# Retention and a two-layer network on one core: what two groups of loads wait for

## Chip, cores, metric

The kernel runs on one core of one Trainium2 chip. The time is the device time of one execution in microseconds (us); the median of several executions is given. A core has five engines: TensorE (PE; its weight loads are listed apart as PEld), VectorE (DVE), ScalarE (ACT), GpSimd (Pool) and SyncE (SP), which issues most of the DMA transfers.

## What is computed

The inputs are q, k and v of shape 4 x 8 x 768 x 64 (batch, heads, sequence, head size), w_in (512 x 2048), w_out (2048 x 512) and alpha (2048), all in fp32. A retention layer feeds a two-layer network:

```
state = gamma[head] * state + outer(k[t], v[t])      # for t = 0..767, per batch and head
y[t]  = (1 / 8) * q[t] @ state                        # gamma[head] = 1 - 2 ** (-5 - head)
x = y as 3072 x 512                                   # token by (head, feature)
h = x @ w_in
g = max(h, 0) + alpha * min(h, 0)
out = g @ w_out                                       # 3072 x 512, fp32
```

## The kernel before

**Units and blocks.** The sequence of each batch is cut into pieces of 256 tokens: 12 units. Two units make a block of 512 tokens, and the network runs block by block, 6 in all.

**A unit** goes through these steps. `load(u)` (L107) issues DMAs on SP that bring k, q and v into staging tiles `ks`, `qs`, `vs` with four buffers each; k and q of units 0 to 3 come in halves of four heads, those of later units whole. `rescale` (L135) multiplies k and q by powers of gamma and writes them as fp16 into `kdq`, on VectorE (V) or on Pool (G); `cast_v` (L148) writes v as fp16. `kdq` is then transposed into `kq`: on TensorE for units 0 to 3 (`turn_pe`, L160, evicted by ScalarE at L174), by a DMA transpose that SP issues for the later ones (`turn_dma`, L156). `score_mm` (L241) multiplies k and q, `masks` (L260) multiplies the two banks of scores by the causal mask on VectorE, one instruction for each bank, `sum_mm` (L190) and `state` (L213) carry the state forward (adding on VectorE, L225; decay on Pool, L226; copies on Pool or ScalarE, L239 and L237), and `out_mm` (L271) makes y, which ScalarE writes into `xT`.

**A block of the network** is `ffn1` (L323: matmuls at L334, ScalarE at L345, VectorE at L347) and `ffn2` (L357: matmuls at L366, eviction on ScalarE at L375, output DMA on SP at L379). Both are generators: `tick(gen, m)` issues the next m of their matmuls, so that the code states by hand which matmul stands between which steps of the units. `ffn2(0)` runs in four parts: its first 16 matmuls use only the first quarter of w_out, the next 16 the second quarter, and so on.

**Weights.** `get_wi` and `get_wo` (L418, L422) issue the weights' DMAs on Pool, which cast fp32 to fp16 on the way. w_out comes in four pieces: `get_wo(0)` to `get_wo(3)`, 512 KB each as written.

**What a load waits for.** `held` is a list with at most one instruction; `hold` (L96) lets the next DMA that `load` issues wait until that instruction has finished (a DMA: until it has landed). Since SP issues in order, the rest of that load, and all that stands behind it on SP, waits too. In the stretch concerned the order on SP is: load(2), load(3), load(4), load(5), transpose of unit 4, load(6), four outputs of block 0, transpose of unit 5, load(7). On Pool it is, among rescales and state copies: get_wo(0), get_wo(1), the rest of unit 2, the state's work of unit 2, get_wo(2), a rescale of unit 3 (`rescale(G, 3, 1, 0, 4)`), get_wo(3), the rest of unit 3, the state's work and the rescales of unit 4 and so on.

Before the change, load(3) is held by get_wo(1) (L504), and load(4), with load(5) behind it, by get_wo(3) (L530).

Of the kernel before, what the change touches and what calls it, by code (L numbers as in the profile page):

```python
# [20 lines left out]
def kernel(  # L21
# [10 lines left out]
    nc = tc.nc  # L32
# [61 lines left out]
    held = []  # L94

    def hold(ins):  # L96
        if held:
            tc.add_manual_dep(
                ins.ins,
                held.pop().ins.name,  # L100
                mybir.DependencyInfo(
                    mybir.DependencyClass.Sync, mybir.DependencyReason.DATA
                ),
                reason="loads behind weights",
            )

    def load(u, parts="kqv"):  # L107
        b, c = divmod(u, UPB)
        t = staged.setdefault(u, {})
        for nm in parts:  # L110
            src = {"k": k, "q": q, "v": v}[nm[0]]
            if nm[0] not in t:
                t[nm[0]] = sbp.tile(
                    [128, H, 2 * D], FP, tag=f"{nm[0]}s", bufs=4, name=f"{nm[0]}s{u}"
                )
            h = slice(0, H) if len(nm) == 1 else slice(4 * int(nm[1]), 4 * int(nm[1]) + 4)
            hold(
                nc.sync.dma_start(  # L118
                    out=t[nm[0]][:, h, :],
                    in_=src[b, h, U * c : U * c + U, :].rearrange(  # L120
                        "h (p r) d -> p h (r d)", r=2
                    ),
                )
            )
# [10 lines left out]
    def rescale(eng, u, t, h0, h1):  # L135
        kdq = unit(u)[0]
        at = OQ * t
        eng.tensor_tensor(  # L138
            out=kdq[:, t, :, h0:h1, :].rearrange("p r h d -> p h r d"),
            in0=staged[u]["kq"[t]][:, h0:h1, :].rearrange("p h (r d) -> p h r d", r=2),  # L140
            in1=tab[:, at + 2 * h0 : at + 2 * h1]
            .rearrange("p (h r) -> p h r", r=2)
            .unsqueeze(3)
            .to_broadcast([128, h1 - h0, 2, D]),
            op=MULT,
        )
# [13 lines left out]
    def turn_pe(u, hh, bank):  # L160

        kdq, kq, _ = unit(u)
        trb = ps(bank, "trb", F16, 1024)
        n = 0
        for t in range(2):
            for r in range(2):
                for p in (2 * hh, 2 * hh + 1):
                    nc.tensor.transpose(  # L168
                        out=trb[:, n : n + 128],
                        in_=kdq[:, t, r, 2 * p : 2 * p + 2, :].rearrange("p a d -> p (a d)"),  # L170
                        identity=ident,
                    )
                    n += 128
        nc.scalar.activation(  # L174
            out=kq.rearrange("p (x a) i -> p x a i", x=4)[:, :, 2 * hh : 2 * hh + 2, :],
            in_=trb.rearrange("p (x a i) -> p x a i", x=4, a=2),
            func=COPY,
            bias=0.0,
            scale=1.0,
        )  # L180
# [60 lines left out]
    def score_mm(u, hh, banks):  # L241
        _, kq, _ = prepped[u]
        kv = kq.rearrange("p (t r a) i -> p t r a i", t=2, r=2)
        scs = [ps(banks[0], "sca"), ps(banks[1], "scb")]
        for r in range(2):
            for pp in range(2):
                p = 2 * hh + pp
                for c in range(2):
                    for a in range(2):
                        at = 256 * r + 128 * pp  # L250
                        nc.tensor.matmul(  # L251
                            out=scs[a][rows(c), at : at + 128],
                            lhsT=kv[rows(a), 0, r, p, rows(c)],
                            rhs=qmove(kq, a, c, p),
                            start=True,
                            stop=True,
                        )
        live[u, hh] = scs

    def masks(u, hh, parts=(0, 1)):  # L260
        for a in parts:
            m2 = sbp.tile([128, 2, 2, 128], F16, tag=f"m2{a}{hh}", bufs=2, name=f"m2{a}{hh}")
            nc.vector.tensor_tensor(  # L263
                out=m2,
                in0=live[u, hh][a].rearrange("p (r a i) -> p r a i", r=2, a=2),
                in1=mask.unsqueeze(2).to_broadcast([128, 2, 2, 128]),
                op=MULT,
            )
            live[u, hh][a] = m2

    def out_mm(u, banks, evict=True):  # L271
        _, kq, vx = prepped[u]
        ys = [ps(banks[0], "y0"), ps(banks[1], "y1")]
        inter = [(u, c) in tgs for c in range(2)]
        assert inter == [u % UPB > 0, True]

        for c in range(2):
            for p in range(NP):
                if inter[c]:
                    nc.tensor.matmul(  # L280
                        out=ys[c][:, 128 * p : 128 * p + 128],
                        lhsT=tgs[u, c][:, p, :],
                        rhs=kq.rearrange("p (t r a) i -> p t r a i", t=2, r=2)[
                            :, 1, :, p, rows(c)
                        ],
                        start=(p == 0),
                        stop=False,
                        skip_group_check=True,
                    )
        for p in range(NP):  # L290
            m2s = live[u, p // 2]
            for r in range(2):
                for c in range(2):
                    for a in range(2):
                        nc.tensor.matmul(  # L295
                            out=ys[c][rows(a), 128 * p : 128 * p + 128],
                            lhsT=vx[rows(c), 2 * p + a, r, :],
                            rhs=m2s[a][rows(c), r, p % 2, :],
                            start=(r == 0 and p == 0 and not inter[c]),
                            stop=(r == 1),  # L300
                            skip_group_check=True,
                        )
        live[u] = ys
        if evict:
            take_y(u, (0, 1))
# [116 lines left out]
    def get_wo(i):  # L422
        s = slice(4 * i, 4 * i + 4)
        return nc.gpsimd.dma_start(out=w_out_all[:, s, :], in_=wo[:, s, :])
# [22 lines left out]
    for t in tgbuf:  # L447
# [16 lines left out]
        out=aps[:, 0:NFT], in_=alpha_sb, identity=tab[0:NFT, OI : OI + NFT]  # L464
    )
    masks(0, 0)
    V.tensor_scalar(
        out=oma_sb, in0=aps[:, 0:NFT], scalar1=-1.0, scalar2=1.0, op0=MULT, op1=ADD
# [4 lines left out]
    sum_mm(0, (6, 7))  # L473
    keep(4, 1)
    masks(0, 1, (0,))
    state(0, 0, V, "aa")
    masks(0, 1, (1,))
    s01 = state_sum(0, 1, G)
    held.append(get_wi(4, 8))
# [21 lines left out]
    keep(5, 6)  # L501
    get_wo(0)
    rescale(G, 2, 0, 0, 4)
    held.append(get_wo(1))  # L504
    load(3, ("k0", "q0", "k1", "q1", "v"))
    rescale(G, 2, 1, 0, 4)
    rescale(G, 2, 0, 4, 8)
    rescale(G, 2, 1, 4, 8)
# [8 lines left out]
    turn_pe(2, 0, 5)  # L517
    tick(gen, 5)
    score_mm(2, 0, (6, 7))
    masks(2, 0)  # L520
    turn_pe(2, 1, 4)
    tick(gen, 8)
    score_mm(2, 1, (6, 7))
    sum_mm(2, (5, 4))
    state(2, 0, G, "ga")
    masks(2, 1)
    get_wo(2)
    rescale(V, 3, 0, 0, 4)
    rescale(G, 3, 1, 0, 4)
    held.append(get_wo(3))  # L530
    load(4)
    load(5)
    rescale(V, 3, 0, 4, 8)
    rescale(G, 3, 1, 4, 8)
    cast_v(G, 3)
# [99 lines left out]
```

## Time and profile before

| | |
|---|---|
| median of 3 runs | 212.51 us (212.19 to 213.4) |
| the profiled execution | 212.42 us |
| its span, first to last instruction | 210.7 us |
| TensorE matmuls busy in the span | 202.3 us (96%) |
| VectorE, ScalarE, Pool busy | 119.5, 98.7, 80.5 us |
| DMA moved | 33.91 MB, 161 GB/s on average |

The profile is that of one execution. Times in it count from its first instruction. A row of the timeline gives start, duration, engine, line, operation, output and inputs, count, and in brackets how long the engine had been idle and what ended that; rows with a count above 1 are merged. "SPq" and "POOLq" are the sequencers that issue DMAs; a DMA's row there is its issue, not its transfer. "issue to landing" is the time from the issue until the data is there. In the DMA views q1 is the queue of SP's transfers and q0 that of Pool's; shares are of all 16 DMA engines and can come out a little over 100%.

### The profile page before, as it was taken

The numbers are of one execution on the slowest core, as the hardware profiler recorded it, in microseconds if no ns is written. First come the engines' busy times: TensorE is split into PE (matmuls) and PEld (weight loads), VectorE is DVE, ScalarE is ACT, GpSimd is POOL, SyncE is SP. The second block draws the span as 40 slices with busy tenths as digits, with TensorE's granted clock in tenths as the row PEclk, the third lists the DMA queues.
The fourth block names the chain that finished last, engine by engine and source line by source line (L and its number), as shares of the span: only waits on it lengthen the run. The fifth ranks groups of instructions, "written<-read, shape, count | busy, mean of one in ns | idle before, by whom it ended". The sixth has DMA issues, their size and how long they took to land.

```text
span 210.7 us, 4991 instructions
## 1 busy us (share of the span) xinstructions
PE 202.3 (96%) x2090; PEld 106.4 (50%) x2090; DVE 119.5 (57%) x196; ACT 98.7 (47%) x160; POOL 80.5 (38%) x102
## 2 busy tenths in 40 slices
PE   7789999989999999999999999999999999999993
PEld 2457545574564555444555444555444555444462
DVE  7785985554288731488750488740588640588000
ACT  2375665361666133666133566133665133665121
POOL 2388055630793699000499300499000610000000
PEclk9999999999999999999999999999999999999999
DMA  6999997994999997599521699421630111100112
GB/s 163 335 226 149 202 281 153 261 189 100 344 248 281 306 277 250 145 288 260 159 101 53 152 294 270 154 82 53 172 78 0 52 55 50 50 0 3 50 71 79
DMA packets 62406, 33.91 MB, mean 161 GB/s; under 512 B 18080, under 2 KB 59440, under 8 KB 62384
## 3 DMA queue, kind: packets, MB, share of 16 engines
q1 hardware_dynamic: 57840, 29.30, 49.0%
q0 software_dynamic: 4224, 4.19, 12.6%
q8 instruction: 16, 0.26, 0.5%
q10 hardware_dynamic: 320, 0.10, 0.3%
q14 instruction: 6, 0.05, 0.1%
HBM read 27.30 MB, written 6.29 MB: 159 GB/s over the span
## 4 chain that ended last, share of the span: by engine, by line
PE 82%; DMA 10%; POOL 2%; DVE 2%; SPq 1%; ACT 1%; issue 1%; DVEq 0%; POOLq 0%
PE hps L334 38%; PE ops L366 33%; DMA wout<-in_moe_w_out_dram 4%; DMA kq<-kdq 3%; PE y L295 2%; DMA ks<-in_k_dram 2%; PE sca L251 2%; PE ops L389 2%; PE y L280 2%; PE st L201 2%; SPq L118 1%; POOL tf L226 1%; DVE ss L225 1%; PE scb L251 1%; PE kps L87 1%
## 5 line engine op out<-in xcount | busy, mean ns | idle before, releaser
L347 DVE SCALAR_TENSOR_TENSOR gt<-hm,oma,hps 128x512 f16<-128x512 f32 (+1 forms) x108 | 73.0, 687 | 47.7 <-ACT hm L345 38.7
L366 PE MATMUL ops<-wout,gt 128*128 128x512 f16 x368 | 83.7, 379 | 0.8 <-DMA wout<-in_moe_w_out_dram 0.8
L334 PE MATMUL hps<-xT,win 128*128 128x512 f16 (+1 forms) x432 | 84.3, 355 | 0.0
L345 ACT ACTIVATE hm<-hps 128x512 f32<-128x512 f32 x96 | 57.3, 597 | 26.4 <-PE hps L334 26.3
L334 PEld LDWEIGHTS <-win 128*128 128x128 f16 x432 | 42.2, 98 | 40.7
L366 PEld LDWEIGHTS <-gt 128*128 128x128 f16 x368 | 34.5, 98 | 41.1 <-issue 0.9
L375 ACT ACTIVATE os<-ops 128x512 f32<-128x512 f32 x23 | 13.6, 598 | 52.3 <-PE ops L366 52.3
L226 POOL TENSOR_TENSOR tf<-ss,tab 128x256 f32<-128x256 f32 x16 | 10.2, 637 | 42.4 <-DVE ss L225 41.8
L263 DVE TENSOR_TENSOR m<-sca,mi 128x512 f16<-128x512 f32 x24 | 16.4, 684 | 17.1 <-PE scb L251 17.1
L239 POOL CAST tg<-tf 64x256 f16<-64x256 f32 x35 | 13.8, 394 | 25.7 <-DVE tf L222 24.0
L313 ACT ACTIVATE xT<-y 128x512 f16<-128x512 f32 x24 | 16.2, 740 | 11.1 <-PE y L295 11.1
L138 POOL TENSOR_TENSOR kdq<-qs,tab 128x1024 f16<-128x1024 f32 (+1 forms) x13 | 20.4, 1569 | 1.8 <-DMA qs<-in_q_dram 1.7
L138 POOL TENSOR_TENSOR kdq<-ks,tab 128x1024 f16<-128x1024 f32 (+1 forms) x10 | 17.3, 1728 | 9.4 <-DMA ks<-in_k_dram 9.1
L263 DVE TENSOR_TENSOR m<-scb,mi 128x512 f16<-128x512 f32 x24 | 16.3, 679 | 0.0
L154 POOL CAST vx<-vs 128x1024 f16<-128x1024 f32 (+1 forms) x13 | 12.6, 971 | 7.5 <-DMA vs<-in_v_dram 7.5
L174 ACT ACTIVATE kq<-trb 128x1024 f16<-128x1024 f16 x8 | 8.2, 1023 | 5.4 <-PE trb L168 5.2
L225 DVE TENSOR_TENSOR ss<-tf,st 128x256 f32<-128x256 f32 x16 | 6.6, 414 | 5.6 <-PE st L201 4.7
L251 PE MATMUL sca<-kq 64*64 64x128 f16 x192 | 8.2, 218 | 1.5 <-ACT kq L174 1.3
L87 PE MATMUL kps<-spin 128*128 128x512 f16 x25 | 7.7, 443 | 1.8 <-DVE spin L432 1.5
L251 PEld LDWEIGHTS <-kq 64*64 64x64 f16 x384 | 6.1, 106 | 4.6 <-ACT kq L174 3.0
L251 PE MATMUL scb<-kq 64*64 64x128 f16 x192 | 8.3, 219 | 0.0
L295 PE MATMUL y<-m,vx 64*64 64x128 f16 x384 | 7.7, 219 | 0.0
(33 smaller groups left out, 69.1 us busy)
## 6 DMA issues: line engine op xcount, KB each, us to landing
out_dram<-os SPq DMA_DIRECT2D x23, 256.0 KB, 2.1
vs<-in_v_dram SPq DMA_DIRECT2D x10, 512.0 KB, 6.7
ks<-in_k_dram SPq DMA_DIRECT2D x8, 512.0 KB, 4.4
qs<-in_q_dram SPq DMA_DIRECT2D x8, 512.0 KB, 5.3
ks<-in_k_dram SPq DMA_DIRECT2D x8, 256.0 KB, 4.4
qs<-in_q_dram SPq DMA_DIRECT2D x8, 256.0 KB, 4.6
win<-in_moe_w_in_dram POOLq DMA_DIRECT2D x4, 512.0 KB, 6.6
wout<-in_moe_w_out_dram POOLq DMA_DIRECT2D x4, 512.0 KB, 9.0
```

Source lines behind the costliest of these rows:

```text
L138: eng.tensor_tensor(out=kdq[:, t, :, h0:h1, :].rearrange("p r h d -> p h r d"), in0=staged[u]["kq"[t]][:, h0:h1, :].rearrange("p h (r d) - ...
L154: eng.tensor_copy(out=o, in_=i)
L226: eng.tensor_tensor(out=t, in0=ss, in1=dec, op=MULT)
L239: nc.gpsimd.tensor_copy(out=o, in_=i)
L251: nc.tensor.matmul(out=scs[a][rows(c), at : at + 128], lhsT=kv[rows(a), 0, r, p, rows(c)], rhs=qmove(kq, a, c, p), start=True, stop=True,)
L263: nc.vector.tensor_tensor(out=m2, in0=live[u, hh][a].rearrange("p (r a i) -> p r a i", r=2, a=2), in1=mask.unsqueeze(2).to_broadcast([128, ...
L313: nc.scalar.activation(out=xT[n][:, ul, :, 128 * c : 128 * c + 128].rearrange("k a (p r) -> k a r p", r=2), in_=ys[c].rearrange("k (a r p) ...
L334: nc.tensor.matmul(out=hps[:, f, :].rearrange("p (u t) -> p u t", t=U), lhsT=w_in_all[:, hp, 128 * (f0 + f) : 128 * (f0 + f) + 128], rhs=x ...
L345: nc.scalar.activation(out=hm, in_=hps, func=RELU, bias=0.0, scale=-1.0)
L347: nc.vector.scalar_tensor_tensor(out=gt[:, f0 + f, U * lo : U * hi], in0=hm[:, f, :], scalar=oma_sb[:, f0 + f : f0 + f + 1], in1=hps[:, f, :],
L366: nc.tensor.matmul(out=opss[tq], lhsT=gt[:, ft, 128 * tq : 128 * tq + 128], rhs=w_out_all[:, ft, :], start=(ft == 0), stop=(ft == NFT - 1),)
L375: nc.scalar.activation(out=os_sb, in_=opss[tq], func=COPY, bias=0.0, scale=1.0)
```

## The change

load(3) is no longer held by `get_wo(1)` but by VectorE's first mask instruction of unit 2, and its call stands behind that mask. load(4) and load(5) are held by `get_wo(2)` instead of `get_wo(3)`, and their calls stand between those two pieces. `masks` returns its last instruction for this purpose. No instruction is added or removed, and the order on SP, on Pool and on VectorE stays what it was.

```diff
@@ masks
-            nc.vector.tensor_tensor(
+            i = nc.vector.tensor_tensor(
...
             live[u, hh][a] = m2
+        return i
@@ the first block
     rescale(G, 2, 0, 0, 4)
-    held.append(get_wo(1))
-    load(3, ("k0", "q0", "k1", "q1", "v"))
+    get_wo(1)
     rescale(G, 2, 1, 0, 4)
...
     score_mm(2, 0, (6, 7))
-    masks(2, 0)
+    held.append(masks(2, 0, (0,)))
+    load(3, ("k0", "q0", "k1", "q1", "v"))
+    masks(2, 0, (1,))
     turn_pe(2, 1, 4)
...
     masks(2, 1)
-    get_wo(2)
+    held.append(get_wo(2))
+    load(4)
+    load(5)
     rescale(V, 3, 0, 0, 4)
     rescale(G, 3, 1, 0, 4)
-    held.append(get_wo(3))
-    load(4)
-    load(5)
+    get_wo(3)
     rescale(V, 3, 0, 4, 8)
```

## Prediction

> **What bounds the kernel now.** I read the page first: its span, and TensorE's share of it.
>
> ```profile
> span 210.7 us, 4991 instructions
> ...
> PE 202.3 (96%) x2090; PEld 106.4 (50%) x2090; DVE 119.5 (57%) x196; ACT 98.7 (47%) x160; POOL 80.5 (38%) x102
> ```
>
> TensorE (PE) is busy for 202.3 of 210.7 us, so only its idle time can be won. The change neither adds nor removes an instruction, so it can only move idle time. Where is there some after the start-up? The view by stages (columns: stretch, its length, busy time of each engine with its count, clock, DMA share, GB/s) says:
>
> ```profile
> 34.00:48.00 14.00, 13.18 (x173) 8.74 (x162) 7.78 (x15) 6.89 (x10) 6.23 (x8) 1.00 0.89 192
> 48.00:77.00 29.00, 28.80 (x372) 15.82 (x373) 16.15 (x29) 12.75 (x22) 17.55 (x21) 1.00 0.97 254
> 77.00:206.00 129.00, 129.00 (x1197) 64.19 (x1187) 68.68 (x102) 58.94 (x98) 38.99 (x45) 1.00 0.42 123
> ```
>
> PE idles 0.82 us in 34 to 48, 0.20 us in 48 to 77, and nothing from 77 to 206. Two waits must be behind this. The view of waits between 30 and 80 us (total, times, longest) names them, the last two rows being one wait, seen by the weight loads and by the matmuls:
>
> ```profile
> PE ops L366 <- DMA wout<-in_moe_w_out_dram: 0.8, 1, 0.8
> ...
> PEld L251 <- DMA kq<-kdq: 0.4, 1, 0.4
> PE sca L251 <- DMA kq<-kdq: 0.2, 1, 0.2
> ```
>
> The chain that ended last (start, us, what) passes through both:
>
> ```profile
> 38.44 0.34 POOL tg L239
> 38.78 8.83 DMA wout<-in_moe_w_out_dram
> ...
> 69.66 6.94 DMA kq<-kdq
> ```
>
> The first is w_out's third piece, get_wo(2): issued at 38.78, once Pool has copied a state, and landed at 38.78 + 8.83 = 47.61. The second is unit 5's DMA transpose, issued by SP at 69.66, landed at 76.60. What each costs is read from the timeline of PE (start, us, engine, line, operation, count):
>
> ```profile
> 44.90 0.62 PE L168 MATMUL trb<-mi,kdq 128*128 128x128 f16 x8
> 45.35 1.04 PE L334 MATMUL hps<-xT,win 128*128 128x256 f16 x8
> 46.23 0.61 PE L168 MATMUL trb<-mi,kdq 128*128 128x128 f16 x8
> 47.65 2.10 PE L366 MATMUL ops<-wout,gt 128*128 128x512 f16 x9 [0.82 <-DMA wout<-in_moe_w_out_dram]
> ...
> 50.31 1.90 PE L366 MATMUL ops<-wout,gt 128*128 128x512 f16 x8
> ```
>
> Eight transposes take 45.35 - 44.90 = 0.45 us of the array when nothing stops what follows. After the second eight, L366 could start at 46.23 + 0.45 = 46.68; it starts at 47.65. **Stall 1 costs 0.97 us.** For stall 2 I take the weight loads' 0.4 us, since matmuls can't start before their weights; so unit 5's transposed tile is due at 76.64 - 0.4 = 76.24 and comes 0.4 us late.
>
> **Part 1: load(3) is held by a mask instead of by w_out's second piece.** SP's timeline, and VectorE's first mask of unit 2:
>
> ```profile
> 36.27 0.37 SPq L118 DMA_DIRECT2D ks<-in_k_dram  x1
> ...
> 50.17 0.37 SPq L118 DMA_DIRECT2D ks<-in_k_dram  x1
> ...
> 59.43 3.56 SPq L158 DMA_TRANSPOSE kq<-kdq  x1
> ...
> 65.32 4.24 SPq L379 DMA_DIRECT2D out_dram<-os  x4
> 69.66 4.21 SPq L158 DMA_TRANSPOSE kq<-kdq  x1
> ```
>
> ```profile
> 34.26 0.69 DVE L263 TENSOR_TENSOR m<-sca,mi 128x512 f16<-128x512 f32 x1 [0.65 <-PE scb L251]
> ```
>
> The mask ends at 34.26 + 0.69 = 34.95, so load(3) goes out at about 35.0 instead of 36.27: all its five DMAs 1.27 us earlier, in the same order. Behind the waiting DMA SP has only load(4) and load(5), which wait longer anyway, and no work ahead of the mask needs load(3). The second piece, which loses its waiter, has landed by 36.27, when load(3) is now let go.
>
> An earlier unit 3 gives PE nothing directly: no wait for unit 3 stands in the rows above. What it does is end its traffic 1.27 us earlier, and there stands the third piece. Traffic by queue, q1 being SP's and q0 Pool's (packets, MB, share of 16 engines), first from 29.99 to 32.00, then from 39.00 to 42.00:
>
> ```profile
> q1 hardware_dynamic: 1387, 0.70, 114.9%
> q0 software_dynamic: 2, 0.00, 0.3%
> ```
>
> ```profile
> q1 hardware_dynamic: 1764, 0.88, 101.6%
> ```
>
> In the first stretch the second piece was already issued and q0 moved 2 packets while unit 2's loads filled the engines. In the second the third piece had been issued at 38.78, and q0 has no row at all: from 39 to 42 only load(3) moves. Twice a piece of w_out begins when the load ahead of it has drained. So I let the third piece begin, and land, 1.27 us earlier: 47.61 - 1.27 = 46.34, against the 46.68 at which PE wants it. The price from both sides: nothing won, if the piece starts late for another reason; 0.97 won, if it is on time. It can't win more, since PE arrives at 46.68 either way. I take **0.97**, the end nearest to the two rows, with 0.34 us to spare.
>
> The Trainium skill speaks against this: "DMA: Bandwidth & Descriptors", section "Queues, rings and completion order", says that each DMA engine takes turns between the queues that have work, a packet at a time. By it the third piece would have moved between load(3)'s packets from the start, load(3)'s lead would bring it little, and the sum would be near rival A's. The row of 39 to 42 has no packet of q0, so the trace so far does not show such turns.
>
> **Part 2: load(4) and load(5) are held by the third piece instead of the fourth.** Pool's order doesn't change: get_wo(2), a rescale of unit 3, get_wo(3), as load() issues on SP alone. Pool's timeline:
>
> ```profile
> 40.90 0.80 POOL L424 DMA_DIRECT2D wout<-in_moe_w_out_dram  x1
> ...
> 51.83 0.39 POOL L239 CAST tg<-tf 64x256 f16<-64x256 f32 x1 [5.12 <-DVE tf L222]
> 54.05 1.90 POOL L138 TENSOR_TENSOR kdq<-ks,tab 128x1024 f16<-128x1024 f32 x1 [1.83 <-DMA ks<-in_k_dram]
> ...
> 57.50 1.90 POOL L138 TENSOR_TENSOR kdq<-qs,tab 128x1024 f16<-128x1024 f32 x1
> ```
>
> load(4) now leaves SP at 50.17 and its k lands in time for Pool at 54.05, that is 3.88 us later. In the new order it leaves at 46.34, 3.8 us earlier, and its k is there by 46.34 + 3.88 = 50.2; if the last of the fourth piece holds it up by 1 us, by 51.2. Pool is free at 51.83 + 0.39 = 52.22, less PE's 0.97, as the cast's input comes through PE: 51.25. So Pool's rescale of unit 4 starts at about 51.3 instead of 54.05, the q half follows after the same 3.45 us (57.50 - 54.05), and the transpose of unit 4, which SP issues at 59.43 as that half ends, moves to about 56.9. From there to unit 5's transpose SP takes 69.66 - 59.43 = 10.2 us of issuing: one transpose, load(6), four outputs. The outputs leave back to back in 4.24 us, so none waits for its data, and I keep the 10.2 us: unit 5's transpose leaves at 67.1 and, after its 6.94 us, lands at 74.0. PE wants it at 76.24 - 0.97 = 75.3. **Stall 2 goes: 0.40.** It takes only 0.4 us of the 2.5 us by which it moves.
>
> What hides the cost of part 2 is the fourth piece's slack. Issued at 40.90, it has landed by 50.17, when load(4) is let go. PE first needs it for the 49th matmul of ffn2(0), the last of the eight at 50.31: 50.31 + 7/8 x 1.90 = 51.97, or 51.0 with PE 0.97 earlier. Behind a third piece that comes 1.27 us earlier it lands at 50.17 - 1.27 = 48.9, and load(4)'s packets meet its tail only. How the two queues share then is seen from 24 to 28 us, where Pool's queue was at work first (w_in's last pieces, then w_out's first) and unit 2's load came in behind:
>
> ```profile
> q1 hardware_dynamic: 550, 0.27, 33.6%
> q0 software_dynamic: 555, 0.55, 84.4%
> ```
>
> Pool's queue, there first, kept 84.4% of 16 engines. So I cost this at nothing, up to a delay of 51.0 - 48.9 = 2.1 us.
>
> **Sum.** The profiled execution took 212.42 us, 1.72 more than its span of 210.7; the median of the runs shown is 212.51, 0.09 above it. 212.42 - 0.97 - 0.40 = 211.05. After 77 us nothing is given back, as PE has no idle time there, and a PE that comes 1.4 us earlier meets loads and transposes that come earlier too. I forecast **211.1 us**.
>
> **Rivals.**
>
> A. *The third piece starts late for its own reason* (its issue, its descriptors, or turns between queues), and not because load(3) is in the way. For it: only two coincidences speak for mine, and the spare time is 0.34 us. Against it: the empty q0 from 39 to 42. Then it lands at 47.61, stall 1 stays, and load(4) goes at 47.65, still 2.5 us early; its k lands at 51.5, Pool starts at 52.2, 1.8 us early, and stall 2 goes all the same. 212.42 - 0.40 = 212.0.
>
> B. *Slower: the loads starve the fourth piece.* If load(4)'s packets stop its tail, as load(3)'s stopped the third piece from 39 to 42, PE stands at the 49th matmul. It decides from a landing after 51.0 us. Load(3), let go at 36.27, fills the engines until 42: at most 5.7 us. With load(4), of the same size, wholly ahead, the fourth piece lands at 48.9 + 5.7 = 54.6 at the latest and PE loses 3.6 us: 211.05 + 3.6 = 214.7; with equal turns, half of the 5.7, it loses 0.75: 211.8. Against it: the row of 24 to 28, and that the piece is a good deal ahead.
>
> C. *SP gives the lead back.* Its 10.2 us are DMA issues that wait for room in the rings; if these stretch by over 1.2 us, stall 2 stays: 212.42 - 0.97 = 211.45.
>
> D. *The change doesn't do what it says*: the mask comes no earlier than the second piece, or the third lands with the fourth. The mask's row says 34.95 against 36.27, so the first can't well be; 212.4.
>
> **How the numbers follow.** Forecast 0.56, A 0.23, B 0.08, C 0.09, D 0.04. A change under 0.5% (1.06 us) is about what a measurement of this kernel can't tell from none. The forecast lies at 0.64%, close above; I give it 0.9 of its chance for faster, C a small part of its own, and a part-won stall 1 lies in A's neighbourhood. Faster 0.52, same 0.38, slower 0.10. The range takes in the forecast with 0.4 us below it, A and C; the costly half of B is left out: 210.6 to 212.9.
>
> **What would show it.** Right: load(3) leaves SP at 35.0; q0 starts near 41; L366 follows the transposes at 46.7 without a wait; load(4) leaves at 46.3; the transposes of units 4 and 5 leave at 57 and 67, and no wait for kq at 75; span 209.3. Wrong: the third piece still landing at 47.6 (A); a wait of L366 near 51 (B); unit 5's transpose landing after 75.3 (C).

## The result, and the profile after

| | before | after |
|---|---|---|
| median of 20 runs | 213.27 us | 211.69 us |
| ratio, 95% interval | | 0.9937 (0.9913 to 0.9962) |

The kernel became faster by 0.63%. A few executions take longer than the rest (4 of the 20 before, 1 of the 20 after); the ratio here and all ratios below leave them out, and without them the medians are 213.08 and 211.67 us. The forecast, 211.1 us against the profiled 212.42, was a ratio of 0.9938. In microseconds it came out 0.6 us low, because it starts from one execution of 212.42 us, which is 0.66 us below that median. Both kernels scatter by more than a microsecond from execution to execution, much of it in the start-up: in the profiles below, ffn2's first matmul comes anywhere from 32.5 us to 34.6 us. So stretches and waits are compared between profiles, and not moments.

The changed kernel was profiled in two more runs, the first two under "Experiments". The rows here are from the second of them (span 210.0 us; line numbers behind `masks` are one higher than before); where the first differs, it is said. First the stages again (columns as in the prediction):

```profile
34.00:48.00 14.00, 13.92 (x177) 9.01 (x176) 9.03 (x15) 6.64 (x11) 6.33 (x8) 1.00 1.00 206
48.00:77.00 29.00, 29.00 (x381) 16.06 (x380) 17.41 (x32) 13.74 (x24) 17.87 (x21) 1.00 1.05 288
77.00:206.00 129.00, 129.00 (x1181) 64.40 (x1180) 68.06 (x102) 58.62 (x97) 38.68 (x45) 1.00 0.39 115
```

PE's idle time is 0.08 us from 34 to 48 (before: 0.82) and nothing from 48 to 77 (before: 0.20). Between 30 and 80 us, no row of PE in the view of waits names a DMA any more, in either profile. SP's timeline shows both changes of the gates, and unit 5's transpose:

```profile
35.64 0.37 SPq L118 DMA_DIRECT2D ks<-in_k_dram  x1
...
46.84 0.37 SPq L118 DMA_DIRECT2D ks<-in_k_dram  x1
...
57.56 1.81 SPq L158 DMA_TRANSPOSE kq<-kdq  x1
...
61.84 4.43 SPq L380 DMA_DIRECT2D out_dram<-os  x4
66.37 4.36 SPq L158 DMA_TRANSPOSE kq<-kdq  x1
```

load(3) leaves at 35.64; the mask that lets it go is the first row here, and ends at 34.92 + 0.69 = 35.61 (this execution's start-up was some 0.7 us later than that of before):

```profile
34.92 0.69 DVE L263 TENSOR_TENSOR m<-sca,mi 128x512 f16<-128x512 f32 x1 [0.65 <-PE scb L251]
35.53 0.68 DVE L263 TENSOR_TENSOR m<-scb,mi 128x512 f16<-128x512 f32 x1
```

Pool issues the third piece 3.81 us behind load(3) instead of 2.51 (before: 38.78 - 36.27), and its landing frees load(4) at 46.84:

```profile
39.45 0.81 POOL L425 DMA_DIRECT2D wout<-in_moe_w_out_dram  x1
40.27 1.05 POOL L138 TENSOR_TENSOR kdq<-qs,tab 128x512 f16<-128x512 f32 x1
41.26 0.80 POOL L425 DMA_DIRECT2D wout<-in_moe_w_out_dram  x1
...
51.87 1.90 POOL L138 TENSOR_TENSOR kdq<-ks,tab 128x1024 f16<-128x1024 f32 x1
```

The piece takes 46.82 - 39.45 = 7.4 us from issue to landing; before it took 8.8. The view of DMA issues has this directly (size, us to landing), first before, then after:

```profile
wout<-in_moe_w_out_dram POOLq DMA_DIRECT2D x1, 512.0 KB, 8.8
```

```profile
wout<-in_moe_w_out_dram POOLq DMA_DIRECT2D x1, 512.0 KB, 7.4
```

So on PE nothing stands between the transposes and the matmul that reads the piece:

```profile
46.89 0.61 PE L168 MATMUL trb<-mi,kdq 128*128 128x128 f16 x8
47.33 2.11 PE L367 MATMUL ops<-wout,gt 128*128 128x512 f16 x9
```

47.33 - 46.89 = 0.44 us, the plain pace of eight transposes; before it was 1.42. In the other profile of the changed kernel a part of stall 1 is left, 48.15 - 47.40 = 0.75, less 0.45 of pace: 0.30 us.

```profile
47.40 0.61 PE L168 MATMUL trb<-mi,kdq 128*128 128x128 f16 x8
48.15 2.10 PE L367 MATMUL ops<-wout,gt 128*128 128x512 f16 x9
```

From ffn2's first matmul to PE's last one, before took 207.16 - 32.48 = 174.68 us and after 206.45 - 33.15 = 173.30: 1.38 us less, where the prediction had 0.97 + 0.40 = 1.37. In the other profile it is 207.26 - 33.70 = 173.56, 1.12 us less.

### The profile page after: what moved, and what is told of

It reads as the page before. It is cut to its first block, busy times and chain, and to the rows that moved or that the text cites. A ratio compares the mean times of both kernels' runs of the same rounds, so it can differ in the third digit from the quotient of the medians.

```text
span 216.4 us, 4989 instructions
## 1 busy us (share of the span) xinstructions
PE 209.5 (97%) x2090; PEld 108.6 (50%) x2090; DVE 121.2 (56%) x196; ACT 98.7 (46%) x160; POOL 80.9 (37%) x102
## 4 chain that ended last, share of the span: by engine, by line
PE 94%; DVE 2%; POOL 1%; ACT 1%; issue 1%; DVEq 0%
PE hps L335 40%; PE ops L367 39%; PE y L296 3%; PE kps L87 3%; PE y L281 2%; PE sca L251 2%; PE ops L390 2%; PE st L201 2%; PE trb L168 1%; DVE m L263 1%; PE scb L251 1%; POOL vx L154 1%; ACT kq L174 0%; POOL tf L226 0%; DVE ss L225 0%
## 5 line engine op out<-in xcount | busy, mean ns | idle before, releaser
L335 PE MATMUL hps<-xT,win 128*128 128x512 f16 (+1 forms) x432 | 87.7, 365 | 0.0
L367 PE MATMUL ops<-wout,gt 128*128 128x512 f16 x368 | 86.9, 391 | 0.0
L335 PEld LDWEIGHTS <-win 128*128 128x128 f16 x432 | 43.0, 100 | 43.3
L367 PEld LDWEIGHTS <-gt 128*128 128x128 f16 x368 | 35.2, 100 | 42.3
L226 POOL TENSOR_TENSOR tf<-ss,tab 128x256 f32<-128x256 f32 x16 | 10.2, 637 | 48.3 <-DVE ss L225 47.3
L87 PE MATMUL kps<-spin 128*128 128x512 f16 x25 | 8.8, 494 | 1.8 <-DVE spin L433 1.5
```

The costliest lines, as they stand in the source:

```text
L87: nc.tensor.matmul(out=pt, lhsT=spin[:, 0:128], rhs=spin, start=True, stop=True)
L335: nc.tensor.matmul(out=hps[:, f, :].rearrange("p (u t) -> p u t", t=U), lhsT=w_in_all[:, hp, 128 * (f0 + f) : 128 * (f0 + f) + 128], rhs=x ...
L367: nc.tensor.matmul(out=opss[tq], lhsT=gt[:, ft, 128 * tq : 128 * tq + 128], rhs=w_out_all[:, ft, :], start=(ft == 0), stop=(ft == NFT - 1),)
```

## Experiments

**The changed kernel**, unaltered, twice.

> The changed kernel, unaltered, for a profile at full clock and a time beside the parts. Theory T (w_out's third piece begins when load(3) has drained): load(3) leaves SP at about 35.0 us, the third piece lands near 46.3, no wait of L366 there, unit 5's DMA transpose leaves near 67, no wait for kq near 75; span about 209.3, ratio to the kernel before about 0.9935. Rival A (the third piece starts by its own issue alone): it still lands at about 47.6, L366 still waits, only the transpose's wait is gone; ratio about 0.998.

> The changed kernel once more, on the chip of this call, for a second profile at full clock. Ratio about 0.993; the third piece lands 7.7 to 8.2 us after its issue instead of some 8.7, L366 waits 0 to 0.3 us, no wait for kq near 75.

Measured: ratios 0.9928 (0.9897 to 0.9959) and 0.9947 (0.9917 to 0.9976). The third piece landed 8.1 and 7.4 us after its issue. In the first profile PE came to the matmul that reads the piece 0.30 us later than by its pace, in the second on time; no wait for kq in either. The kernel before, once more:

> The kernel before, unaltered, as a control and for a second profile. Ratio 1.000 within its interval. Both theories: L366 waits 0.6 to 1.0 us for the third piece, which lands some 8.7 us after its issue, and the weight loads wait some 0.4 us for unit 5's transpose; the start-up, up to ffn2's first matmul, may differ by up to 1 us from the first profile.

Measured: ratio 1.0018 (0.9984 to 1.0052). Its profiled execution took 216.9 us and gives no second profile to compare with. So what stalls 1 and 2 cost in the kernel before as a rule rests on its one profile and on the kernels below that keep one of the two holds.

**Each part alone.** Part 1 alone:

```diff
-    held.append(get_wo(1))
-    load(3, ("k0", "q0", "k1", "q1", "v"))
+    get_wo(1)
...
-    masks(2, 0)
+    held.append(masks(2, 0, (0,)))
+    load(3, ("k0", "q0", "k1", "q1", "v"))
+    masks(2, 0, (1,))
```

> Part 1 alone: load(3) held by the mask, load(4) and load(5) by the fourth piece as before. Theory T: the third piece lands near 46.3 and stall 1 (0.97 us) goes; the fourth lands 1.27 us earlier too, at about 48.9, load(4) leaves then, and unit 5's transpose lands at about 76.60 - 1.27 = 75.3, just when the earlier PE wants it, so nearly all of stall 2 goes with it: 1.2 to 1.4 us faster, ratio about 0.994. Rival A: stall 1 stays; load(4) leaves as before, stall 2 stays: ratio 1.000.

Measured: 0.9953 (0.9919 to 0.9987). The third piece landed 7.7 us after its issue, and no wait for w_out is left. Of stall 2 there remained:

```profile
PEld L251 <- DMA kq<-kdq: 0.2, 1, 0.2
```

Half of it, that is, as load(4) came no earlier than the fourth piece's landing at 49.84.

Part 2 alone (run twice):

```diff
-    get_wo(2)
+    held.append(get_wo(2))
+    load(4)
+    load(5)
     rescale(V, 3, 0, 0, 4)
     rescale(G, 3, 1, 0, 4)
-    held.append(get_wo(3))
-    load(4)
-    load(5)
+    get_wo(3)
```

> Part 2 alone: load(3) held by the second piece as before, load(4) and load(5) by the third. Both theories: the third piece still lands at about 47.6 and stall 1 stays; load(4) leaves at 47.65 instead of 50.17, unit 5's transpose about 1.8 us earlier, stall 2 (0.40 us) goes: ratio about 0.998. If the earlier loads starve the fourth piece (rival B), L366 waits near 52 and the ratio is above 1.

> Part 2 alone once more, beside the kernel with the moved transpose: its first ratio was 0.9947 (0.9915 to 0.9978), where stall 2 alone would give 0.998. If 0.998 is right, this run comes out near it and the two runs together include it; if part 2 holds something more, it comes out near 0.995 again.

Measured: 0.9947 (0.9915 to 0.9978) and 0.9991 (0.9955 to 1.0028); their middle, 0.997, is near the 0.998 of stall 2, and the first run by itself was misleading. In the first profile PE's waits show stall 1 still there and stall 2 gone; this is the row:

```profile
PE ops L366 <- DMA wout<-in_moe_w_out_dram: 0.6, 1, 0.6
```

In the second profile the wait for kq was back with 0.4 us of the weight loads: there load(4) left early, at 48.25, but its k landed 6.8 us after its issue instead of 3.8. So part 2 alone removes stall 2 in some executions and not in all.

**Stall 2 by other means.** Nothing moves but unit 5's transpose on SP:

```diff
     cast_v(G, 5)
+    turn_dma(5)
     tick(gen, 8)
     out_mm(3, (6, 7))
     tick(gen)
-    turn_dma(5)
     load(7)
```

> The kernel before, with one move on SP alone: the transpose of unit 5 goes ahead of block 0's four outputs instead of behind them. All loads and weights wait as before, so stall 1 stays. The transpose leaves near 65.3 us instead of 69.66 and lands near 71 or 72, well before PE wants it (76.24): stall 2 goes and nothing else changes. If stall 2 is worth its 0.40 us, the ratio is about 0.998. If the loads' earlier start in part 2 was worth more than stall 2 alone, this kernel stays above part 2's ratio.

Measured: 0.9978 (0.9937 to 1.0019), near what was expected, but the interval includes no change, so the ratio alone doesn't show it. The transpose left at 65.94 and landed at 74.24; PE's waits name w_out alone, with 1.5 us in this execution:

```profile
PE ops L366 <- DMA wout<-in_moe_w_out_dram: 1.5, 1, 1.5
```

The rows of waits give idle time, which for stall 1 is some 0.15 us less than the prediction's measure (0.82 against 0.97 before). By that measure, start to start less the 0.45 us of pace, the profiles so far compare like this (us; "lead" is from load(3)'s issue to the third piece's, "stretch" from ffn2's first matmul to PE's last):

| | lead | third piece takes | stall 1 | stall 2 | stretch |
|---|---|---|---|---|---|
| before | 2.51 | 8.8 | 0.97 | 0.4 | 174.68 |
| part 2 alone, first | 2.12 | 8.6 | 0.78 | 0 | 174.05 |
| part 2 alone, second | 2.55 | 8.4 | 0.54 | 0.4 | 174.24 |
| unit 5's transpose first | 2.40 | 9.5 | 1.69 | 0 | 175.00 |
| part 1 alone | 3.80 | 7.7 | 0 | 0.2 | 173.50 |
| changed kernel, first | 3.80 | 8.1 | 0.30 | 0 | 173.56 |
| changed kernel, second | 3.81 | 7.4 | 0 | 0 | 173.30 |

Stall 1 thus varies from 0.5 to 1.7 us in the four profiles with load(3) behind the second piece. And in every profile the two stalls account for the stretch: what it differs by from before's 174.68 is what the stalls differ by, within 0.05 us. The kernel with the moved transpose, for one, lost 0.72 to stall 1 and won 0.40 from stall 2, and its stretch is 0.32 longer. That shows stall 2's size where the ratios can't.

**Does load(3) delay the third piece?** load(3) later, the rest as before:

```diff
-    held.append(get_wo(1))
-    load(3, ("k0", "q0", "k1", "q1", "v"))
+    get_wo(1)
...
-    masks(2, 1)
+    held.append(masks(2, 1, (0,)))
+    load(3, ("k0", "q0", "k1", "q1", "v"))
+    masks(2, 1, (1,))
```

> As before, but load(3) is held by the first mask of unit 2's second half, which ends at about 38.2 us: load(3) leaves some 2 us later than before, about when the third piece is issued (38.8). Theory T: the third piece waits for load(3)'s end and lands some 2 us later, near 49.6; PE waits about 3 us for it instead of 0.97, and the kernel takes some 2 us more, ratio about 1.009. Rival A: the third piece lands at about 47.6 as before or earlier; only unit 3's rescales come later, which costs PE at most some 0.6 us: ratio 1.000 to 1.003.

Measured: 1.0248 (1.0205 to 1.0292), worse than either theory. SP, Pool and VectorE of this kernel:

```profile
39.82 0.37 SPq L118 DMA_DIRECT2D ks<-in_k_dram  x1
40.23 0.51 SPq L118 DMA_DIRECT2D qs<-in_q_dram  x1
40.79 0.52 SPq L118 DMA_DIRECT2D ks<-in_k_dram  x1
41.35 0.51 SPq L118 DMA_DIRECT2D qs<-in_q_dram  x1
```

```profile
40.36 0.81 POOL L425 DMA_DIRECT2D wout<-in_moe_w_out_dram  x1
43.51 1.03 POOL L138 TENSOR_TENSOR kdq<-qs,tab 128x512 f16<-128x512 f32 x1 [2.34 <-DMA qs<-in_q_dram]
44.49 0.80 POOL L425 DMA_DIRECT2D wout<-in_moe_w_out_dram  x1
54.67 1.03 POOL L138 TENSOR_TENSOR kdq<-qs,tab 128x512 f16<-128x512 f32 x1 [9.37 <-DMA qs<-in_q_dram]
```

```profile
42.64 0.69 DVE L138 TENSOR_TENSOR kdq<-ks,tab 128x512 f16<-128x512 f32 x1 [2.25 <-DMA ks<-in_k_dram]
50.98 0.69 DVE L138 TENSOR_TENSOR kdq<-ks,tab 128x512 f16<-128x512 f32 x1 [7.64 <-DMA ks<-in_k_dram]
```

The third piece, issued at 40.36, did take longer: 10.4 us, to 50.72. But the greater loss lies with load(3): its first halves of k and q came in 3 us, its second halves only at 50.95 and 54.59, right behind the third piece (50.72) and the fourth (54.41). VectorE and Pool stood for them, and PE with them:

```profile
52.51 1.03 PE L168 MATMUL trb<-mi,kdq 128*128 128x128 f16 x8 [5.89 <-DVE gt L348]
```

The row names VectorE's ffn1 step as the releaser; what had come last is the rescale at 50.98, just ahead of it on VectorE, by its 7.64 us of waiting. A theory that only the pieces wait for the loads is wrong: it goes both ways.

**The same with whole DMAs.**

```diff
-    load(3, ("k0", "q0", "k1", "q1", "v"))
+    load(3)
```

> As the kernel with the late load(3), in which k's and q's second halves landed right behind w_out's third and fourth piece (50.95 behind 50.72, 54.59 behind 54.41) and PE stood 5.9 us, but load(3) in three whole DMAs (k, q, v) instead of five. Theory T2 (the two queues take turns by whole DMA): k is through ahead of the third piece (near 44), q lands right behind the third piece (near 51) and v behind the fourth (near 54); q is needed whole, so PE stands for about 2.5 us instead of 5.9: ratio about 1.010. If the queues share byte by byte instead, the same megabyte of k and q is ready as late as in halves, near 54.6: ratio about 1.025, as before.

Measured: 1.0018 (0.9977 to 1.0058), 5 us faster than in halves. It decides against an even sharing of bytes, under which nothing would have changed. Turns by whole DMA, as I had them, fail in the order: q landed at 45.76, ahead of the third piece (48.46) and not behind it, and v at 49.42, ahead of the fourth (52.51), which Pool here issued only at 46.82. With five DMAs PE stood 5.89 us for unit 3's rescales, with three 1.44 us (1.10 and 0.34). How much of that is due to the halves themselves isn't separated: with the whole q Pool also issued the fourth piece 2.3 us later (46.82 against 44.49), as its rescale ahead of it had to wait longer. By which rule the engines choose stays open.

**load(3) far ahead**, held by nothing (against the changed kernel):

```diff
-    held.append(masks(2, 0, (0,)))
     load(3, ("k0", "q0", "k1", "q1", "v"))
-    masks(2, 0, (1,))
+    masks(2, 0)
```

> As the changed kernel, but load(3) is held by nothing: SP issues it right behind load(2), near 24.4 us, long before w_out's second piece (29.2) and third (38.8). Theory T: the second piece now waits for load(3)'s end, near 36.5, and lands near 40.8 instead of 36.3, while PE wants it at 37.7: PE waits some 3 us; the third piece, with nothing ahead of it but the second, takes less than the 8.8 us from issue to landing that it took before. About 3 us slower than the changed kernel, ratio to the kernel before about 1.008. Rival A (turns between the queues): the second piece lands at most 1.5 us later, near 37.8, without a wait worth naming; ratio about 0.994.

Measured: 0.992 (0.9886 to 0.9954). load(3) left at 26.17 us, and when the third piece was issued, at 38.85, SP's queue had 0.34 MB of its 1.57 MB left to move (before: 1.21 MB). The third piece took the shortest time of all profiles from issue to landing:

```profile
wout<-in_moe_w_out_dram POOLq DMA_DIRECT2D x1, 512.0 KB, 6.1
```

The second piece was late, as theory T had it, but PE's wait was half of the 3 us that it gave; the piece landed at 39.28, and PE stood for it:

```profile
39.33 1.46 PE L367 MATMUL ops<-wout,gt 128*128 128x512 f16 x6 [1.41 <-DMA wout<-in_moe_w_out_dram]
```

That the ratio is yet as good as the changed kernel's isn't explained by this profile, which was the slowest of this kernel's ten executions (212.73 us, their median being 211.57). How long the second piece is usually waited for here stays open.

**load(4) and load(5) held by nothing**, right behind load(3) (against the changed kernel; the case of rival B at its worst):

```diff
-    held.append(get_wo(2))
+    get_wo(2)
     load(4)
     load(5)
```

> As the changed kernel, but load(4) and load(5) are held by nothing: SP issues them right behind load(3), from 37.5 us on, around the issue of the third piece (38.8). Theory T: 4.5 MB of SP's queue stand ahead of the third piece; at 0.3 MB per us they drain near 51, it lands near 56 instead of 46.3, and PE waits some 9 us: ratio about 1.04. Turns between the queues (the rule weighed in the prediction): the third piece gets every second packet and lands near 49, PE waits 2 to 3 us: ratio 1.005 to 1.01.

Measured: 1.0023 (0.9987 to 1.006). PE stood for the third piece, which took 9.3 us with 3 MB of SP's queue behind load(3):

```profile
48.11 1.24 PE L367 MATMUL ops<-wout,gt 128*128 128x512 f16 x5 [1.31 <-DMA wout<-in_moe_w_out_dram]
```

Theory T, taken at its word (the piece starts when SP's queue has drained), wanted a landing near 56; it came at 48.07. From 44 to 48 us both queues moved, packet for packet (packets, MB, share):

```profile
q0 software_dynamic: 564, 0.56, 83.3%
q1 hardware_dynamic: 553, 0.28, 34.4%
```

**A version with the third piece early** (against the changed kernel).

```diff
     cast_v(G, 2)
+    get_wo(2)
...
-    held.append(get_wo(2))
+    held.append(get_wo(3))
     load(4)
     load(5)
     rescale(V, 3, 0, 0, 4)
     rescale(G, 3, 1, 0, 4)
-    get_wo(3)
```

> As the changed kernel, but Pool issues w_out's third piece right behind unit 2's last cast (near 34.7 us instead of 39), and load(4) and load(5) wait for the fourth piece, which is issued near 41. The third piece then lands near 42, long before PE wants it; the fourth near 47. Both theories: no wait for w_out and none for kq; all that can be won over the changed kernel is what is left of stall 1 (0.1 to 0.3 us): ratio about 0.992, not to be told from the changed kernel's.

Measured: 0.999 (0.9954 to 1.0026): no gain over before, and none of the changed kernel's. In its profile the third piece was issued at 37.25, 0.22 us behind load(3) and with the second piece still under way (it landed at 38.71). The piece landed after 7.4 us, at 44.69, and it was load(3) that waited: its second halves landed at 45.88 and 48.28, PE stood 0.34 and 0.29 us for VectorE's and Pool's rescales of unit 3, and the fourth piece freed load(4) no earlier than before, at 50.65. No version was found that is clearly faster than the changed kernel.

## Why the prediction was right

- **Part 1, the gate.** load(3) leaves as the mask ends, 1.3 us further ahead of the third piece (3.81 us against 2.51). Right.
- **Part 1, stall 1 (0.97 us).** It goes, but not always whole: 0.30 and 0.0 us are left in the two profiles of the changed kernel, none in that of part 1 alone. The size was that of the one profile; in others of its kind stall 1 is 0.5 to 1.7 us. That the forecast's ratio meets the measured one to the fourth digit is luck.
- **Part 1, the reason.** Right in its direction, too strong in its words. With no other piece under way and load(4) held, the third piece takes the shorter, the longer load(3)'s lead over its issue: 0.5 us of lead 10.4 us (9.1 in whole DMAs); 2.1 to 2.6 us of lead 8.4 to 9.5, over four profiles; 3.8 us 7.4, 7.7 and 8.1. With load(3) out long before it took 6.1. The version with the third piece early doesn't fit this: 0.2 us of lead and 7.4 us. There the second piece was still moving, so the lead alone doesn't decide it. I had taken the 1.27 us whole; against before's 8.8 the three profiles give 0.7, 1.1 and 1.4. Against rival A: before, from 2.4 to 3.1 us behind the piece's issue (41.2 to 41.9), SP's queue has the engines alone; after, from 2.5 to 3.05 us (41.95 to 42.5), the piece moves with 58.6%.

```profile
q1 hardware_dynamic: 425, 0.21, 106.4%
```

```profile
q1 hardware_dynamic: 204, 0.10, 62.1%
q0 software_dynamic: 43, 0.04, 58.6%
```

- **But the piece doesn't wait for the whole queue to drain.** With 3 MB more behind load(3) it took 9.3 us and not the 17 that draining would have cost. The prediction's own row of 24 to 28 us showed it: 550 packets against 555. I read it by its shares of time, as the right of the queue that was there first; but with load(4) and load(5) free SP's queue was there first, and Pool's had 83.3% all the same. In this, the rule of the Trainium skill that I had set aside ("DMA: Bandwidth & Descriptors", section "Queues, rings and completion order": turns between the queues, a packet at a time) agrees with the trace of that kernel, 564 packets against 553 in 4 us, better than my reading did. It doesn't explain the first 2.4 to 3.9 us behind the issue, in which the third piece gets nothing while SP's queue moves load(3) (3.40 before, 2.55 after), nor the second halves of the late load(3).
- **Part 2, stall 2 (0.40 us).** Unit 5's transpose leaves at 66.37 (forecast 67.1; its terms, 51.3 + 3.45 + 1.93 + 10.2, give 66.9) and lands at 72.7 (74.0), and the wait is gone in both profiles of the changed kernel. Its size is borne out by the stretches of the table. Part 1 alone took half of it, where the sum had no part for it.
- **Rival B.** The fourth piece landed at 49.44, before PE's 49th matmul: the last of the eight at 50.00, so 50.00 + 7/8 x 1.90 = 51.7. Load(4), issued at 46.84, didn't make PE wait for it. Rival C: SP's stretch from one transpose to the next was 66.37 - 57.56 = 8.8 us, shorter than the 10.2 I had kept.
- **The sum** was right by its parts (1.37, against 1.38 and 1.12 us from ffn2's start to PE's end); the forecast in microseconds was 0.6 us low because a single profile of before stood for its median.

## What to carry to other kernels

When two DMA queues share the DMA engines, a load that nobody waits for can still decide when the awaited transfer lands: look at what is in the other queue in the microseconds after the awaited one is issued. A gate on a compute step that lies a fixed time ahead of the next weights keeps the two apart (a lead of 3.80 or 3.81 us in the three profiles of the table); a gate on the landing of an earlier transfer moves with it (2.12 to 2.55 us). And starting the awaited transfer earlier is no gain by itself, if it then pushes back loads that are needed just as soon.

## What was not expected of the hardware

- A 512 KB piece of w_out took 5.7 us from issue to landing as the fourth piece of the kernel with the late whole load(3), issued when 0.39 MB of load(3) were left, and 10.4 us as the third piece of the kernel with the late halves, issued when nearly all of load(3) was left.

```profile
wout<-in_moe_w_out_dram POOLq DMA_DIRECT2D x1, 512.0 KB, 5.7
```

- In the two kernels with the late load(3), the small loads suffered more than the large ones when they ran into weights: the half of k issued 0.43 us behind the third piece took 10.2 us, while in whole DMAs q, issued 0.12 us ahead of it, took 6.6 us for twice the bytes. First the half of k of the late load(3), then the whole q:

```profile
ks<-in_k_dram SPq DMA_DIRECT2D x1, 256.0 KB, 10.2
```

```profile
qs<-in_q_dram SPq DMA_DIRECT2D x1, 512.0 KB, 6.6
```
